# Lo parts of weights on the 256-byte grid, hi parts 96 bytes off it, and a dearer adding transfer in the plan

## The chip, the core and the metric

One program runs on one core of one Trainium2 chip. The metric is the device time of one execution in microseconds, and lower is better. Three runs of the kernel before took 527.31, 530.25 and 537.80 us; their median is 530.25 us. TensorE is called PE here, its weight loads PEld, VectorE DVE, ScalarE ACT, GpSimd POOL and SyncE SP.

## The reference

Attention with 2 batches, 12 heads, 448 positions and a head size of 64, whose scores are capped by a tanh, is followed by two feed-forward layers with their own weights, each 768 to 2048 to 768, over all 896 tokens. All is float32.

```python
scores = cap * np.tanh(scale * (q @ k.T) / cap)
x = softmax(scores) @ v                      # 896 x 768 after the heads are put side by side
h = x @ w1_in;  x = (s * np.maximum(h, 0)**2 + b) @ w1_out
h = x @ w2_in;  out = (h * np.clip(h + 3, 0, 6) / 6) @ w2_out
```

## The kernel before, in words

**The attention** runs first, to about 91 us into the span. It is not touched by the change, except that ACT and DVE already unpack the first weight columns beside it.

**The two feed-forward layers** make up the rest. A float32 number is kept as two tiles of the format fp32r that PE reads in one pass: hi is the number rounded, lo is what is left. A product of a weight block and an activation block is three matmuls into one PSUM bank, in `matmuls` (line 300): lo weight by hi activation, hi weight by lo activation, hi weight by hi activation. Each has a weight load of 128 by 128 before it and a moving stream of 448 columns, 1,792 bytes in a partition, one batch's tokens. There are 710 such products, so 2,130 matmuls, all on line 303. The matrix products are taken in a scheme that forms a two-by-two block product from seven products instead of eight; it adds and subtracts blocks of weights on DVE (line 614), and blocks of activations with transfers on POOL's queue that add into their destination (`accumulate`, line 781; there are 52), or on DVE (line 780).

**A weight's way.** A transfer on SP's queue lands it in `raw`; ACT rescales the upper half of the bits (line 285) and ACT or DVE bring the rest (lines 289, 293, 298); the float32 result f is then split by `parts` (line 600): ACT rounds f into a new tile h (line 603), and DVE writes f minus h over f itself (line 604). So h holds the hi part, and f's place becomes the lo part.

**The places in the memory** are handed out by `Space.take` (line 75) in two large areas. Places for 448 columns of activations begin on a grid of `LINE` = 64 elements, 256 bytes, counted from the area's start. All longer places, those of weights, f and h alike, begin `OFFSET` = 24 elements, 96 bytes, off that grid. A block of 128 weight columns is 512 bytes, so each block that PE loads is off the grid by the same 96 bytes, and each moving stream is on it.

**The order of the work** is written by a planner, `Plan.order` (line 125), before the program is built. It plays the tasks through with a cost for each, four queues (PE, DVE, ACT, and one for all transfers) and the memory places, and starts on each engine the ready task with the earliest due time. PE takes its products from a list, and may pull one ahead of up to 35 others that aren't ready. A task of another engine is taken as done `LAG` later than its end. An adding transfer holds the transfer queue for `SUM_COST` and lands `SUM_LATE` after that. The engines then work their instructions off strictly in this written order; the planned times don't exist on the chip.

**The squares** of the first layer's activations (`activation`, line 674) are made by DVE in one instruction (line 690), or, for the column blocks named in `SQUARES`, by ACT in two (lines 687, 688).

Of the kernel before, what the change touches and what calls it, by code (L numbers as in the profile page):

```python
# [16 lines left out]
B, H, S, D = 2, 12, 448, 64  # L17
# [7 lines left out]
BL = HK * 128  # L25
CI = KD * 128
# [3 lines left out]
SCALE = 1.0 / D**0.5  # L30
FIRST = 3
PLAIN = 4
SQUARES = (5, 6, 7, 9, 11)
HEAD = 2.0

NEGATIVE = tuple(range(HK, KD)) + tuple(range(KD, KD + HK))
LOAD = 0.004, 2.5
AHEAD = {"ACT": 30.0}
SUM_COST, SUM_LATE = 1.37, 3.5
STORE_LATE = 3.0  # L40
PIECE = 0.602
SEVENS = 2, 2
# [1 line left out]
LOWS = (True, True, False, False)  # L44

LINE, OFFSET = 64, 24
SPACE = 36 * S + 12 * CI + OFFSET, 49 * S + 6 * CI + OFFSET
OUT_ORDER = (0, 3, 1, 4, 2, 5)


class Res:


    def __init__(self, kind, tile=None, n=S, at=None):
        self.kind, self.tile, self.left, self.held, self.order = kind, tile, 0, tile is not None, None
        self.n, self.at, self.low = n, at, None


class Space:
# [12 lines left out]
                return  # L72
        raise RuntimeError("not free")

    def take(self, n):
        for area in ((1, 0) if n == S else (0, 1)):
            for a, b in self.free[area] if n == S else reversed(self.free[area]):
                at = a + (-a) % LINE if n == S else b - n - (b - n - OFFSET) % LINE
                if a <= at and at + n <= b:
                    self.cut(area, at, n)  # L80
                    return area, at
        return None
# [19 lines left out]
class Plan:  # L102


    LAG = 0.35
    WINDOW = 36

    def __init__(self, sizes):
# [2 lines left out]
    def add(self, engine, cost, run, after=(), use=(), soon=None):  # L111
        t = Task(engine, cost, run, after, list(use), len(self.tasks))
        for u in t.use:
            u.left += 1
        for a in t.after:
            a.then.append(t)
        t.soon = soon
        self.tasks.append(t)
        return t

    def order(self):
# [3 lines left out]
        for t in reversed(self.tasks):  # L125
            for s in t.then:
                t.due = min(t.due, s.due - t.cost - t.late - self.LAG)
        made = {}
# [4 lines left out]
        for t in reversed(self.tasks):  # L133
            if t.engine != "PE":
                for s in t.then:
                    t.due = min(t.due, s.due - t.cost - t.late - self.LAG)
        free = dict(self.sizes)
        space = Space(SPACE, {(*u.at, u.n) for t in self.tasks for u in t.use if u.kind == "mem" and u.held} | set(self.taken))
        banks, seen = 0, {}
# [22 lines left out]
        while left:  # L162
            moved = True
            while moved:
                moved = False
                for e, queue in waiting.items():
                    if idle[e] > now + 1e-9:
                        continue
                    for t in queue[:self.WINDOW] if e == "PE" else queue:
                        if e in AHEAD and now < t.due - AHEAD[e]:  # L170
                            continue
                        if any(a.end is None or a.end + (0 if a.engine == e and e != "DMA" else self.LAG) > now + 1e-9 for a in t.after):
                            continue
                        want = [u for u in t.use if not u.held]
                        need = {}
                        ok = True
                        for u in want:
                            if u.kind == "mem":
                                need[u] = space.take(u.n)
                                ok = need[u] is not None  # L180
                            else:
                                ok = free[u.kind] > 0 and (u.kind != "bank" or u.order == next_bank)
                                if ok:
                                    need[u] = u.kind
                                    free[u.kind] -= 1
                            if not ok:
                                break
                        if not ok:
                            for u, k in need.items():
                                if u.kind != "mem":  # L190
                                    free[k] += 1
                                elif k is not None:
                                    space.give(*k, u.n)
                            continue
                        for u, k in need.items():
                            u.held = True
                            if u.kind == "mem":
                                u.at = k
                            elif k == "bank":
                                next_bank += 1  # L200
                        t.start, t.end = now, now + t.cost + t.late
                        idle[e] = now + t.cost
                        ends.append(t)
                        queue.remove(t)
                        left -= 1
                        moved = True
                        break
            times = [x for x in idle.values() if x > now + 1e-9]
            times += [t.due - AHEAD[e] for e in AHEAD for t in waiting[e] if t.due - AHEAD[e] > now + 1e-9]
            times += [t.end + self.LAG for t in done[-80:] + ends if t.end + self.LAG > now + 1e-9]  # L210
            if not times:
                stuck = {e: [(t.name if hasattr(t, "name") else t.number, [a.number for a in t.after if a.end is None]) for t in q[:3]] for e, q in waiting.items()}
                raise RuntimeError(f"plan stuck at {now}: {free} {stuck}")
            now = min(times)
            for t in [t for t in ends if t.end <= now + 1e-9]:
                ends.remove(t)
                done.append(t)
                for u in t.use:
                    u.left -= 1
                    if u.left == 0 and u.kind == "mem":  # L220
                        space.give(*u.at, u.n)
                    elif u.left == 0:
                        free[u.kind] += 1
# [11 lines left out]
def attention_moe_moe(ctx: ExitStack, tc: tile.TileContext, qk, v, cap, w1i, w1o, s, b, w2i, w2o, out):  # L235
    nc = tc.nc
    placed = [0]
    first_area = ctx.enter_context(tc.tile_pool(name="ma", bufs=1))
    first_area.tile([128, SPACE[0]], F32, name="ma")
    first_area.seal()  # L240
    areas = [nc.sbuf_base - 4 * SPACE[0]]

    def view(at, n, dt=F32):

        placed[0] += 1
        return nc.alloc_sbuf_tensor_at(f"m{placed[0]}", (128, n), dt, offset=areas[at[0]] + 4 * at[1])[:, :]
# [18 lines left out]
    xf = [view(a, S) for a in xf_at]  # L265
    top_of = lambda n: (0, SPACE[0] - n)
    f_at = [top_of((i + 1) * CI) for i in range(FIRST + 1)]
    h_at = [top_of((i + FIRST + 2) * CI) for i in range(FIRST + 1)]
    fa_at, fb_at = top_of(8 * CI + 4 * BL), top_of(8 * CI + 7 * BL)

    def raw_tile():
        return wp.tile([128, CI, 2], U32, name="raw", tag="raw", bufs=3)
# [32 lines left out]
    at = tc.alloc_tile_pool(name="at", bufs=3)  # L305
# [146 lines left out]
    def take(p):  # L452

        xu[p] = xf[p]
        nc.vector.tensor_copy(xu[p], pav.pop(p)[:, :S])
# [70 lines left out]
    def feed_forward():  # L526
# [6 lines left out]
        def res(n=S):  # L533
            return Res("mem", None, n)
# [6 lines left out]
        def low_of(f):  # L541
            if f.low is None:
                f.low = view(f.at, f.n, F32R)
            return f.low
# [7 lines left out]
        def t_of(r, dt=F32):  # L552
            if r.tile is None:
                r.tile = view(r.at, r.n, dt)
            return r.tile
# [44 lines left out]
        def parts(f, after, before=()):  # L600

            h = res(f.n)
            a = add("ACT", acts(f.n), lambda: nc.scalar.copy(t_of(h, F32R), f.tile), after, [f, h])  # L603
            c = add("DVE", dve(f.n), lambda: nc.vector.tensor_sub(low_of(f), f.tile, h.tile.bitcast(F32)), [a, *before], [f, h])  # L604
            return (h, f), [a, c]
# [25 lines left out]
        def out_block(layer, mt, half):  # L631
            f = res(2 * CO)
            g, tasks = parts(f, [convert(w_src(layer, 1, (mt, 2 * half + i)), CO, f, i * CO, low=False) for i in range(2)])
            return g, 0, tasks
# [39 lines left out]
        def activation(layer, f, bi, c_psum, made, c_slot=None):  # L674
# [9 lines left out]
            a = add("ACT", acts(S, layer), relu, made, [src_res, t] if t is not src_res else [t], soon)  # L684
            on_act = layer == 0 and f in SQUARES
            if on_act:
# [324 lines left out]
    with tc.manual_schedule():  # L1011
# [57 lines left out]
        for p in range(P - 2):  # L1069
            at_step(U * (p // 2) + 6 + 3 * (p % 2), take, p)  # L1070
# [85 lines left out]
```

## Time and profile before

| what | value |
|---|---|
| median of three runs | 530.25 us (527.31 to 537.80) |
| profiled execution | 533.35 us, its span 531.6 us |
| PE busy in the span | 519.9 us, 98% |
| weight loads busy | 427.8 us, 80% |
| DVE, ACT, POOL busy | 443.8, 417.8, 46.7 us |
| granted TensorE clock, mean of the span | 0.999 |

A matmul's busy time overlaps the next one's, so 98% says only that PE seldom stands still. The pace at which matmuls follow each other has to be read from the count in a stretch of time.

### The profile page before, as it was taken

To read this page: it belongs to the slowest core of one execution; us is meant where nothing else is said; L and a number is where in the kernel's file an instruction comes from. 1 tells how busy PE (TensorE), PEld (TensorE's weight loads), DVE (VectorE), ACT (ScalarE), POOL (GpSimd) and SP (SyncE) were. 2 spreads that over 40 slices of the span, in tenths; PEclk is the share of its full clock that TensorE was granted. 3 is DMA by queue.
4 is the path that set the end of the run, shared out by engine and by line. 5 is a ranking of instruction groups with operands and counts; after the bars stand their busy time and mean duration, and the time that the engine had idled before them with its cause. 6 is when DMAs were issued, how large, how long until landed. Compare 5 with 4: busy or idle time off the path is not lost.

```text
span 531.6 us, 7389 instructions
## 1 busy us (share of the span) xinstructions
PE 519.9 (98%) x2720; PEld 427.8 (80%) x2720; DVE 443.8 (83%) x673; ACT 417.8 (79%) x574; POOL 46.7 (9%) x62
## 2 busy tenths in 40 slices
PE   8999999999999999999988999999999999999997
PEld 3232335999899999999978998999999999999996
DVE  2789999999987838989979999999866699799732
ACT  6999999698876849899969999854577887799610
POOL 0000000350000000001432210000000000035100
PEclk9999999999999999999999999999999999999999
DMA  8846411794237514325897743222676213279611
GB/s 308 330 124 195 130 36 50 218 190 121 81 113 261 189 51 139 120 80 144 169 288 148 172 111 100 80 80 81 210 258 203 80 48 102 91 188 174 158 56 69
DMA packets 25286, 76.31 MB, mean 144 GB/s; under 512 B 3234, under 2 KB 13218, under 8 KB 25122
## 3 DMA queue, kind: packets, MB, share of 16 engines
q1 hardware_dynamic: 17616, 63.75, 36.3%
q0 software_dynamic: 7488, 11.93, 13.5%
q8 instruction: 21, 0.34, 0.3%
q10 hardware_dynamic: 146, 0.16, 0.1%
q14 instruction: 15, 0.12, 0.1%
HBM read 61.11 MB, written 2.79 MB: 120 GB/s over the span
## 4 chain that ended last, share of the span: by engine, by line
PE 53%; DVE 12%; ACT 7%; issue 3%; DMA 2%; POOL 0%; DVEq 0%; POOLq 0%; ACTq 0%
PE pf L303 24%; PE pav L303 21%; PE pz L303 8%; DMA m<-m 2%; DVE m L298 2%; DVE m L604 2%; DVE m L690 2%; DVE m L704 1%; ACT m L603 1%; ACT m L285 1%; DVE m L793 1%; DVE m L293 1%; ACT raw L289 1%; DVE m L614 1%; DVE m L796 1%
## 5 line engine op out<-in xcount | busy, mean ns | idle before, releaser
L303 PE MATMUL pf<-m,m 128*128 128x448 f32 x1053 | 224.0, 366 | 3.2 <-ACT pf L867 1.6
L303 PEld LDWEIGHTS pf<-m,m 128*128 128x128 f32 x1053 | 197.0, 188 | 21.6 <-ACT pf L867 2.0
L303 PE MATMUL pav<-m,m 128*128 128x448 f32 x813 | 173.6, 365 | 0.5 <-DVE pav L739 0.5
L303 PEld LDWEIGHTS pav<-m,m 128*128 128x128 f32 x813 | 152.3, 188 | 13.9 <-DVE pav L739 0.9
L298 DVE SCALAR_TENSOR_TENSOR m<-raw,m 128x512 uint32<-128x512 uint32 (+1 forms) x123 | 92.4, 764 | 14.1 <-ACT raw L289 12.2
L604 DVE TENSOR_TENSOR m<-m,m 128x1024 fp32r<-128x1024 f32 (+2 forms) x56 | 79.6, 1425 | 15.6 <-ACT m L603 15.5
L603 ACT CAST m<-m 128x1024 fp32r<-128x1024 f32 (+2 forms) x56 | 68.2, 1220 | 27.2 <-DVE m L298 15.8
L781 POOL DMA_DIRECT2D m<-m x52 | 45.9, 943 | 450.1 <-DVE m L692 152.2
L289 ACT ACTIVATE raw<-raw 128x768 uint16<-128x768 uint16 (+1 forms) x37 | 67.9, 1834 | 0.7
L285 ACT ACTIVATE m<-raw 128x512 f32<-128x512 f32 (+1 forms) x79 | 60.0, 766 | 10.7 <-DMA raw<-in_w2o 2.8
L303 PE MATMUL pz<-m,m 128*128 128x448 f32 x264 | 57.7, 366 | 0.2 <-DVE m L604 0.2
L303 PEld LDWEIGHTS pz<-m,m 128*128 128x128 f32 x264 | 49.4, 187 | 4.7 <-DVE m L604 0.5
L293 DVE TENSOR_SCALAR m<-m 128x512 uint32<-128x512 uint32 (+1 forms) x80 | 37.4, 475 | 4.5 <-ACT m L285 4.4
L349 ACT ACTIVATE t<-t 128x896 f32<-128x896 f32 x42 | 39.9, 949 | 1.2
L344 ACT ACTIVATE t<-ps 128x896 f32<-128x896 f32 x42 | 37.8, 901 | 3.6 <-PE ps L336 3.6
L336 PE MATMUL ps<-rqk 64*128 64x448 f32 x144 | 34.1, 576 | 1.1 <-ACT t L344 1.0
L362 PE MATMUL pav<-t,va 128*64 128x448 f32 x144 | 31.9, 555 | 0.2 <-ACT t L349 0.2
L336 PEld LDWEIGHTS ps<-rqk 64*128 64x128 f32 x144 | 11.5, 185 | 22.9 <-ACT t L344 12.8
L614 DVE TENSOR_TENSOR m<-m 128x384 f32<-128x384 f32 (+1 forms) x46 | 26.0, 566 | 1.5 <-PE pf L303 0.7
L362 PEld LDWEIGHTS pav<-t,va 128*64 128x64 f32 x144 | 8.4, 136 | 20.1 <-issue 15.4
L704 DVE SCALAR_TENSOR_TENSOR m<-m,bt,m 128x448 fp32r<-128x448 f32 x32 | 21.5, 681 | 3.3 <-ACT m L698 2.5
L793 DVE SCALAR_TENSOR_TENSOR m<-m,m 128x448 fp32r<-128x448 f32 x31 | 19.0, 620 | 4.7 <-DMA m<-m 2.4
(135 smaller groups left out, 422.8 us busy)
## 6 DMA issues: line engine op xcount, KB each, us to landing
raw<-in_w1i SPq DMA_DIRECT2D x16, 768.0 KB, 5.1
raw<-in_w1o SPq DMA_DIRECT2D x24, 512.0 KB, 3.9
raw<-in_w2i SPq DMA_DIRECT2D x16, 768.0 KB, 5.0
raw<-in_w2o SPq DMA_DIRECT2D x24, 512.0 KB, 4.0
m<-m POOLq DMA_DIRECT2D x52, 224.0 KB, 4.1
rqk<-in_qk SPq DMA_DIRECT2D x11, 448.0 KB, 4.7
out<-m SPq DMA_DIRECT2D x12, 224.0 KB, 1.9
rb<-rows SPq DMA_DIRECT2D x10, 224.0 KB, 3.8
```

Source lines behind the costliest of these rows:

```text
L285: nc.scalar.activation(bits, up, AF.Copy, scale=2.0**-112)
L289: nc.scalar.activation(by[:, :, 2], by[:, :, 1], AF.Copy, scale=2.0**-13, bias=0.5**14 - 0.5)
L293: nc.vector.tensor_scalar(bits, bits, 3, None, op0=ALU.logical_shift_left)
L298: nc.vector.scalar_tensor_tensor(out=bits, in0=part, scalar=29 if low else mask, in1=bits, op0=ALU.logical_shift_right if low else ALU.bit ...
L303: nc.tensor.matmul(ps[:, :S], w[a], rhs[r], start=start and i == 0, stop=stop and i == 2, skip_group_check=True)
L336: nc.tensor.matmul(ps[:, j, :S], raw_qk[p][rows, 1, c * 128:(c + 1) * 128], raw_qk[p][rows, 0, :], start=True, stop=True)
L344: nc.scalar.activation(u_t[n], u_ps.pop(n)[:, :, :S], AF.Tanh, scale=icap_r)
L349: nc.scalar.activation(u_t[n], u_t[n], AF.Exp, scale=cap_r)
L362: nc.tensor.matmul(pav[p][(top, end)[j], :S], va[bi][:, d, (2 * (p % 2) + j) * NC + c, :], u_t[n][:, j, :], start=(p % 2 == 0 and c == 0), ...
L603: a = add("ACT", acts(f.n), lambda: nc.scalar.copy(t_of(h, F32R), f.tile), after, [f, h])
L604: c = add("DVE", dve(f.n), lambda: nc.vector.tensor_sub(low_of(f), f.tile, h.tile.bitcast(F32)), [a, *before], [f, h])
L781: t = add("DMA", SUM_COST, lambda: nc.gpsimd.dma_start(out=r.tile, in_=other.tile, accum_op=ALU.add), after, [r, other])
```

## The change

Places for weights can now be asked for with a shift: `parts` sets 24 elements for h, the hi part, and every other weight place, so f with the later lo part, gets 0 and begins on the 256-byte grid. The early weights, whose places are written out by hand, follow the same rule, for which both areas end 40 elements later. So of each product's three weight loads one (lo) is now on the grid and two (hi) are 96 bytes off it, as before.

In the planner an adding transfer holds the queue for 1.6 instead of 1.37, the lag after another engine's task is 0.4 instead of 0.35, and block 6 of the squares moves from ACT to DVE.

```diff
-SQUARES = (5, 6, 7, 9, 11)
+SQUARES = (5, 7, 9, 11)
...
-SUM_COST, SUM_LATE = 1.37, 3.5
+SUM_COST, SUM_LATE = 1.6, 3.5
...
-SPACE = 36 * S + 12 * CI + OFFSET, 49 * S + 6 * CI + OFFSET
+SPACE = 36 * S + 12 * CI + LINE, 49 * S + 6 * CI + LINE
...
-        self.n, self.at, self.low = n, at, None
+        self.n, self.at, self.low, self.shift = n, at, None, 0
...
-    def take(self, n):
+    def take(self, n, shift):
...
-                at = a + (-a) % LINE if n == S else b - n - (b - n - OFFSET) % LINE
+                at = a + (-a) % LINE if n == S else b - n - (b - n - shift) % LINE
...
-    LAG = 0.35
+    LAG = 0.4
...
-                                need[u] = space.take(u.n)
+                                need[u] = space.take(u.n, u.shift)
...
-    h_at = [top_of((i + FIRST + 2) * CI) for i in range(FIRST + 1)]
-    fa_at, fb_at = top_of(8 * CI + 4 * BL), top_of(8 * CI + 7 * BL)
+    h_at = [top_of((i + FIRST + 2) * CI + LINE - OFFSET) for i in range(FIRST + 1)]
+    fa_at, fb_at = top_of(8 * CI + LINE + 4 * BL), top_of(8 * CI + LINE + 7 * BL)
...
             h = res(f.n)
+            h.shift = OFFSET
```

The new costs move instructions. Two places matter to the prediction.

ACT at the end of the first layer, some 270 to 281 us into the span before, where the last sums of activations are split into hi parts (lines 789 and 792) and a bank is seeded for the next block by a copy (line 867). Before:

```order
L792 ACTIVATE m_2526<-m_2238 128x448
L603 CAST m_2532<-m_2405 128x1536
L982 ACTIVATE m_2548<-pz 128x448
L792 ACTIVATE m_2554<-m_2220 128x448
L982 ACTIVATE m_2561<-pav 128x448
L789 ACTIVATE m_2566<-m_1920,bt 128x448
L982 ACTIVATE m_2570<-pf 128x448
L792 ACTIVATE m_2577<-m_2369 128x448
L982 ACTIVATE m_2584<-pav 128x448
L867 COPY pf<-pf 128x448
```

And with the change, where line numbers from 603 on are one higher:

```order
L793 ACTIVATE m_2527<-m_2225 128x448
L983 ACTIVATE m_2538<-pz 128x448
L790 ACTIVATE m_2545<-m_1900,bt 128x448
L604 CAST m_2552<-m_2389 128x1536
L983 ACTIVATE m_2563<-pav 128x448
L793 ACTIVATE m_2571<-m_2213 128x448
L983 ACTIVATE m_2576<-pf 128x448
L983 ACTIVATE m_2581<-pav 128x448
L868 COPY pf<-pf 128x448
L793 ACTIVATE m_2594<-m_2367 128x448
```

The rounding of a large weight tile (the cast of 1,536 columns) has moved from ahead of the second line to behind the biased split, and one split of a sum has moved from ahead of the seeding copy to behind it.

PE at the same place: products of three matmuls, named by bank, activation and weight tile. Before:

```order
L303 MATMUL pf<-m_2554,m_2348 128x448
L303 MATMUL pf<-m_2575,m_2327 128x448
L303 MATMUL pf<-m_2554,m_2327 128x448
L303 MATMUL pf<-m_2526,m_2348 128x448
L303 MATMUL pf<-m_2537,m_2327 128x448
L303 MATMUL pf<-m_2526,m_2327 128x448
L303 MATMUL pf<-m_2566,m_2418 128x448
L303 MATMUL pf<-m_2582,m_2346 128x448
L303 MATMUL pf<-m_2566,m_2346 128x448
```

And with the change:

```order
L303 MATMUL pf<-m_2527,m_2346 128x448
L303 MATMUL pf<-m_2543,m_2325 128x448
L303 MATMUL pf<-m_2527,m_2325 128x448
L303 MATMUL pav<-m_1968,m_2568 128x448
L303 MATMUL pav<-m_2026,m_2552 128x448
L303 MATMUL pav<-m_1968,m_2552 128x448
L303 MATMUL pf<-m_2571,m_2346 128x448
L303 MATMUL pf<-m_2586,m_2325 128x448
L303 MATMUL pf<-m_2571,m_2325 128x448
```

A product of the next block (into pav, with the weights that the moved cast makes) has come in between the last two products of this group, whose two places are exchanged.

## Rows read from the trace of the kernel before

**Rows 1.** Page: the span and busy time of the engines.
```profile
span 531.6 us, 7389 instructions
PE 519.9 (98%) x2720; PEld 427.8 (80%) x2720; DVE 443.8 (83%) x673; ACT 417.8 (79%) x574; POOL 46.7 (9%) x62
```

**Rows 2.** Page: groups by line; busy us, mean ns of one | idle before.
```profile
L303 PE MATMUL pf<-m,m 128*128 128x448 f32 x1053 | 224.0, 366 | 3.2 <-ACT pf L867 1.6
...
L303 PE MATMUL pav<-m,m 128*128 128x448 f32 x813 | 173.6, 365 | 0.5 <-DVE pav L739 0.5
...
L303 PE MATMUL pz<-m,m 128*128 128x448 f32 x264 | 57.7, 366 | 0.2 <-DVE m L604 0.2
L303 PEld LDWEIGHTS pz<-m,m 128*128 128x128 f32 x264 | 49.4, 187 | 4.7 <-DVE m L604 0.5
```

**Rows 3.** Stretches, line 303 alone: us, PE and PEld busy (count), clock, DMA.
```profile
86.00:329.00 243.00, 235.98 (x1172) 219.17 (x1171) 1.00 0.56 150
330.00:528.00 198.00, 197.75 (x957) 178.84 (x956) 1.00 0.44 125
...
142.00:246.00 104.00, 104.00 (x522) 97.59 (x521) 1.00 0.42 138
252.00:274.00 22.00, 22.00 (x112) 20.65 (x111) 1.00 0.94 221
284.00:328.00 44.00, 44.00 (x222) 41.31 (x222) 1.00 0.59 147
332.00:526.00 194.00, 194.00 (x941) 175.76 (x940) 1.00 0.44 126
```

**Rows 4.** The chain that ended last: start us, us, what.
```profile
162.65 10.80 PE pf L303 x54
...
463.90 9.30 PE pav L303 x45
```

**Rows 5.** Waits of PE: waited for, us in total, times, longest.
```profile
PE pf L303 <- ACT pf L867: 1.6, 1, 1.6
...
PE pf L303 <- DVE m L793: 1.3, 1, 1.3
...
PE pav L303 <- DVE pav L739: 0.5, 1, 0.5
...
PE pf L303 <- ACT m L792: 0.2, 1, 0.2
PE pz L303 <- DVE m L604: 0.2, 1, 0.2
```

**Rows 6.** Timeline of ACT, 270 to 281 us: start, us, instruction, idle before.
```profile
270.96 1.46 ACT L603 CAST m<-m 128x1536 fp32r<-128x1536 f32 x1
...
278.07 0.67 ACT L789 ACTIVATE m<-m,bt 128x448 fp32r<-128x448 f32 x1 [1.72 <-DMA m<-m]
278.65 0.53 ACT L982 ACTIVATE m<-pf 128x448 f32<-128x448 f32 x1
279.17 0.58 ACT L792 ACTIVATE m<-m 128x448 fp32r<-128x448 f32 x1
279.65 0.52 ACT L982 ACTIVATE m<-pav 128x448 f32<-128x448 f32 x1
280.07 0.54 ACT L867 COPY pf<-pf 128x448 f32<-128x448 f32 x1
```

**Rows 7.** Groups of the squares on ACT and DVE, columns as in Rows 2.
```profile
L690 DVE SCALAR_TENSOR_TENSOR m<-m,st 128x448 f32<-128x448 f32 x22 | 14.8, 678 | 0.0
...
L688 ACT ACTIVATE m<-m,st 128x448 f32<-128x448 f32 x10 | 6.7, 670 | 0.3
...
L687 ACT ACTIVATE m<-m 128x448 f32<-128x448 f32 x10 | 5.8, 577 | 0.2
```

**Rows 8.** Page: issues of adding transfers, KB each, median us to landing.
```profile
m<-m POOLq DMA_DIRECT2D x52, 224.0 KB, 4.1
```

## The prediction

> **What bounds the kernel now.** I read the page's busy times first. PE is busy for 519.9 of 531.6 us [rows 1], so only two things can change the time much: the pace of its matmuls, and the few places where it stands still. The groups by line come next: the three groups of line 303 hold 1053 + 813 + 264 = 2,130 matmuls [rows 2], all of one shape, and fill the span from about 86 to 528 us [rows 3]. Their mean duration of 366 ns is no pace, since they overlap.
>
> The pace is read from stretches in which PE never waits. From 142 to 246 us there are 104.0 us and 522 matmuls, where the count takes in those cut by the two ends, about two; so 104.0 / 520 = 0.200 us each. From 332 to 526 us it is 194.0 / 939 = 0.2066 us [rows 3]. The chain of waits says it without ends: 54 matmuls in 10.80 us are 200.0 ns each, 45 in 9.30 us are 206.7 ns [rows 4]. So there are **two paces**, 200.0 and 206.7 ns, and the granted clock is 1.00, the 2.4 GHz level, in both. 1,173 matmuls (2,130 less 957) stand before 329.5 us, nearly all at the fast pace, and 957 behind it at the slow one [rows 3]. Between lies one short wait of PE, for line 604 [rows 5]. After the earlier waits the fast pace came back: 252 to 274 us gives 22.0 / 110 and 284 to 328 us gives 44.0 / 220, both 0.200 [rows 3]. A weight load takes 187 ns [rows 2], and loads are busy for 97.59 of 104 us at the fast pace and 175.76 of 194 us at the slow one [rows 3]: the load is no longer there, only the gap to the next.
>
> The profiled execution took 533.35 us. At the fast pace throughout it would be 957 x 6.7 ns = 6.4 us shorter, 526.95 us; at the slow pace throughout 1,173 x 6.7 ns = 7.9 us longer, 541.2 us. The three runs, 527.31 to 537.80 us, lie between these. I take it that they differ mainly in how long each ran at which pace. The profiled execution lies 3.1 us above the median, so about half of its slow share is typical.
>
> Last, the waits of PE within line 303 sum to 1.6 + 1.3 + 0.5 + 0.2 + 0.2 = 3.8 us [rows 5]; more than that is not to be had from the plan.
>
> **The change, part by part.**
>
> *Places of the lo parts.* Nothing is added to PE: 2,130 loads and 2,130 matmuls remain. 710 of the loads now begin on the grid. The trace has no matmul of line 303 with a weight there, so the price has to be bounded. Nearest from above: every load of the product keeps or takes the slow pace, +7.9 us against the profiled execution. Nearest from below: every matmul runs at the fast pace, -6.4 us. Further down, no row excludes that one more step of 6.7 ns goes from the 710 lo matmuls (-4.8 us more) or from all 2,130 (-14.3 us more); further up the 710 could take one more step, +4.8 us over the slow pace.
>
> I take **-6.4 us**, the fast pace throughout. Places alone don't set the pace, since one set of places showed both; a pace is something that the stream falls into, and it left the slow one after all waits but the last [rows 3]. At the slow pace it stayed for 957 matmuls in a row, each with the same distance between its load's place and its stream's. With the change this distance changes twice in every three matmuls, so a pace that lives from repeating itself has less to hold on to, and 200.0 is the one that was found again more often. That is an inference, not a row, and its chance below is accordingly small.
>
> Against it speaks the Trainium skill, "TensorE: Matmul & The Clock Gate", section "Step-by-step: what each phase is for": PE has two independent SBUF read ports, one for the moving stream and one for weight loads, and loading the next weights takes no read bandwidth from the running matmul. By it the place of a weight changes nothing, and this term of the sum is 0 instead of -6.4 us. The trace neither bears it out nor refutes it, since no load of line 303 has another place.
>
> *Addresses in ACT's and DVE's work.* The same instructions of the same sizes run on f and h; no cost is taken, and DVE has idle time in the span [rows 1].
>
> *SUM_COST and LAG.* These make no instruction; they move some. PE's largest waits, 1.3 us for line 793 and 1.6 us for line 867 [rows 5], lie at one place, 275 to 281 us. Before, ACT stands there for 1.72 us before line 789 until a transfer lands, then needs 0.67 for it, 0.53, 0.58 and 0.52 for three more, and only then comes the seeding copy at 280.07 us [rows 6]. With the change one split (0.58 us) is behind the copy, and PE has a product of the next block to do meanwhile, three matmuls or 0.6 us. But the cast of 1,536 columns, 1.46 us [rows 6], is now between line 789 and the copy, as are one more bank copy (0.52) and one other split (0.58). If line 789 still waits until 278.07 us, the copy comes 1.46 + 0.52 + 0.58 - 0.58 = 2.0 us later, and PE, with 0.6 us of other work, stands 1.4 us longer. If the places handed out anew, or the earlier stand of line 789 in ACT's order, end that wait, up to 3.8 us go. The adding transfers keep their order there, and take a median of 4.1 us to land [rows 8], so nothing makes them earlier by itself. I take **0**, between +1.4 and -3.8, as neither end has the better row. What is late next in the good case is DVE's line 793, whose own 1.3 us of PE's wait [rows 5] stays.
>
> *Squares of block 6.* Two batches: ACT loses 2 x (577 + 670) = 2.5 us, DVE gains 2 x 678 = 1.4 us [rows 7]. PE's only wait near there is 0.5 us for DVE's line 739 [rows 5]; one square of 0.68 us ahead of it would make it 1.2, none would leave it. Bounds -0.5 and +0.7 us, taken as **0**. The cover is PE's list, in which a product's results are used many products later; without it the 1.4 us on DVE would count.
>
> *Sum.* 533.35 - 6.4 + 0 + 0 = 526.95, so **527.0 us**, 0.6% under the median of 530.25 us.
>
> **The rivals.** About 2% of the median, 10.6 us, is what can be told from no change here; so faster means under 519.6 us and slower over 540.9 us.
>
> *Forecast, the fast pace holds: 0.38.* 527.0 us, and with the bounds of the plan's terms 523 to 529 us.
>
> *The place of a weight does nothing: 0.31.* The change then doesn't do what it says, the two paces share the matmuls by chance as before, and the time lies between 525 and 540 us, most likely near the median, 530 us. For it: one set of places showed both paces [rows 4]. Against it: nothing in the rows. This is the rule of "TensorE: Matmul & The Clock Gate" on the two read ports.
>
> *A pace below 200 ns: 0.17.* If the 710 lo matmuls lose one more step the time is 526.95 - 4.8 = 522.2 us; if all do, 512.7 us. For it: a load takes only 187 ns [rows 2], so 13 ns of each 200 are neither load nor needed by the next load. Against it: no stretch without a wait ran under 0.200 us [rows 3]. The Trainium skill, same page, section "Back-to-back issue gap", gives columns / 2.4 + 2.5 ns for matmuls that follow each other, which is 189.2 ns for 448 columns; by that estimate the time would be 526.95 - 2,130 x 10.8 ns = 503.9 us. The rows disagree with it at both paces.
>
> *Slower, the lo loads drag the stream into the slow pace: 0.14.* The place is each product's first matmul: its load from the grid runs beside a moving stream on the same grid. If these two meet, one step of 6.7 ns is lost there, and the stream stays at the slow pace for the next two, as it did for 957 matmuls [rows 3]. All slow gives 541.2 us; with one step more for the 710 it is 546.0 us. It decides from the point where more than the lo third is slow: the third alone, 710 x 6.7 = 4.8 us over 526.95, is 531.7 us, no change. Against it: with the old places the stream also left the slow pace.
>
> **How the numbers follow.** The predicted time is the forecast's 527.0 us. Under 513.5 us lies the all-lower case with the page's, about 0.10; over 538.5 us lie the slow rival's upper part and the far end of the second case, about 0.11. So the range is 513.5 to 538.5 us. The forecast's own range is 523 to 529 us. Faster by over 2%: from the third case the part in which all matmuls lose a step, 0.11, and 0.03 for that together with a gain in the plan, so 0.14. Slower: the dragged stream at 541.2 us or more, 0.09, since a part of it ends just under the bound. Within 2%: 0.77.
>
> **What would show it.** In stretches without a wait, line 303 counts 0.200 us a matmul everywhere, 332 to 526 us included, where it was 0.2066. If a stretch there shows 0.2066 again, the second case holds; 0.2022 (one slow in three) or 0.1978 (one faster in three) would show that the place of the load itself has a price. For the plan's terms: PE's waits for lines 793 and 867, now 794 and 868, are again together 2 to 4 us, and the cast of 1,536 columns stands ahead of the seeding copy. The prediction is wrong if a pace other than the two appears, or if PE's waits sum to more than 6 us.

## The result and the profile after

Over 20 runs the changed kernel took a median of 533.61 us (530.35 to 537.10). Run beside it, the kernel before took 535.00 us (20 runs, 527.31 to 537.94; the 530.25 us shown ahead of the prediction was a median of three). The ratio that belongs to the verdict is 1.0058 [1.0034, 1.0083]: no change by the measure of 2%, and slower by a little, where the prediction had faster by a little. That ratio leaves out runs over 1.5% above the fastest of the same kernel, which takes 10 of the 20 runs of before and none of the change's, so I set all runs beside it: with those of the later experiments, 44 of the change have a mean of 533.43 us and 136 of before 533.57 us, ratio 0.9997 [0.9982, 1.0013]. The kernels are equal in the mean; they differ in how their runs spread. Before's fall into two groups, 59 of 136 under 532.5 us (mean 529.75) and nearly all others at 534 to 540 (mean 536.50); of the change's, 17 of 44 are under 532.5.

The profiled execution of the changed kernel took 530.96 us, so it belongs to the lower group. The page's span and busy times, against [rows 1]:
```profile
span 529.2 us, 7398 instructions
PE 515.2 (97%) x2720; PEld 428.2 (81%) x2720; DVE 446.0 (84%) x675; ACT 415.8 (79%) x570; POOL 46.8 (9%) x62
```
The groups of line 303, against [rows 2]; busy us, mean ns of one | idle before:
```profile
L303 PE MATMUL pf<-m,m 128*128 128x448 f32 x1041 | 219.2, 363 | 2.5 <-DVE m L605 1.6
...
L303 PE MATMUL pav<-m,m 128*128 128x448 f32 x825 | 174.2, 363 | 2.7 <-DVE m L605 2.1
...
L303 PE MATMUL pz<-m,m 128*128 128x448 f32 x264 | 57.0, 363 | 1.0 <-DVE m L605 1.0
L303 PEld LDWEIGHTS pz<-m,m 128*128 128x128 f32 x264 | 49.5, 188 | 4.5 <-DVE m L605 1.4
```
The 2,130 matmuls are there again. A load takes 188 ns, 187 before. Stretches without a wait, line 303 alone, columns as in [rows 3]:
```profile
222.00:246.00 24.00, 24.00 (x122) 22.53 (x121) 1.00 0.37 115
...
400.00:440.00 40.00, 40.00 (x202) 37.56 (x201) 1.00 0.42 143
...
480.00:524.00 44.00, 44.00 (x222) 41.31 (x221) 1.00 0.52 115
```
With the two that the ends cut taken off, 40.00 / 200 and 44.00 / 220 are 0.200 us: in this execution the stretch after 332 us, 0.2066 before [rows 3], runs at the fast pace. The chain of waits agrees, against [rows 4] (start us, us, what):
```profile
463.49 8.40 PE pav L303 x42
...
479.69 9.60 PE pf L303 x48
```
That is 200.0 ns both times. The waits of PE within line 303, against [rows 5]:
```profile
PE pav L303 <- DVE m L605: 2.1, 1, 2.1
PE pf L303 <- DVE m L605: 1.6, 1, 1.6
...
PE pz L303 <- DVE m L605: 1.0, 1, 1.0
...
PE pf L303 <- DVE m L797: 0.5, 1, 0.5
PE pav L303 <- DVE pf L740: 0.2, 1, 0.2
PE pf L303 <- DVE pav L740: 0.2, 1, 0.2
PE pf L303 <- ACT pf L868: 0.2, 1, 0.2
PE pav L303 <- DVE m L744: 0.2, 1, 0.2
```
They sum to 6.0 us, 3.8 before [rows 5]. The waits for lines 868 (the seeding copy) and 794 have nearly gone, and DVE's line 605, the lo parts of a weight, is late in their place, three times. The timeline of ACT at the same place, against [rows 6]:
```profile
275.81 0.67 ACT L790 ACTIVATE m<-m,bt 128x448 fp32r<-128x448 f32 x1 [0.20 <-DMA m<-m]
276.38 1.46 ACT L604 CAST m<-m 128x1536 fp32r<-128x1536 f32 x1
...
281.06 0.56 ACT L868 COPY pf<-pf 128x448 f32<-128x448 f32 x1
```
The transfer that held line 789 until 278.07 us now lets line 790 begin at 275.81; the cast stands ahead of the seeding copy as foretold, and the copy comes 1.0 us later than before (281.06 after 280.07), but PE waits only 0.2 us for it. The longest of the waits for line 605 lies here too. PE's product of the next block, which the prediction counted as work to do meanwhile, needs the lo parts that DVE makes behind the moved cast:
```profile
278.19 1.75 DVE L605 TENSOR_TENSOR m<-m,m 128x1536 fp32r<-128x1536 f32 x1
279.99 0.88 PE L303 MATMUL pav<-m,m 128*128 128x448 f32 x3 [2.15 <-DVE m L605]
```

### The profile page after: what moved, and what is told of

The parts are those of the page before. It is cut to its first block, busy times and chain, and to the rows that moved or that the text cites. A ratio compares the mean times of both kernels' runs of the same rounds, so it can differ in the third digit from the quotient of the medians.

```text
span 529.2 us, 7398 instructions
## 1 busy us (share of the span) xinstructions
PE 515.2 (97%) x2720; PEld 428.2 (81%) x2720; DVE 446.0 (84%) x675; ACT 415.8 (79%) x570; POOL 46.8 (9%) x62
## 5 line engine op out<-in xcount | busy, mean ns | idle before, releaser
L303 PE MATMUL pf<-m,m 128*128 128x448 f32 x1041 | 219.2, 363 | 2.5 <-DVE m L605 1.6
L303 PEld LDWEIGHTS pf<-m,m 128*128 128x128 f32 x1041 | 194.8, 188 | 18.1 <-DVE m L605 2.0
L303 PEld LDWEIGHTS pav<-m,m 128*128 128x128 f32 x825 | 154.6, 188 | 14.4 <-DVE m L605 2.5
L793 ACT ACTIVATE m<-m 128x448 fp32r<-128x448 f32 x31 | 17.9, 585 | 9.1 <-PE pav L303 5.7
```

The source lines that it names most:

```text
L303: nc.tensor.matmul(ps[:, :S], w[a], rhs[r], start=start and i == 0, stop=stop and i == 2, skip_group_check=True)
```

## What a run's time is made of

I took 20 executions apart by the starts of their 2,130 matmuls: how many run at a slow pace and by how much; the stops, which are all that lies between neighbouring starts beyond 200 ns and isn't pace (the 3.6 us near 88 us in which PE does other matmuls are left out); and matmuls that follow at 373 ns, while the granted clock is 0.50 (the 1.2 GHz level), 0.173 us too long each. What is left is 521.0 to 522.5 us in all of them, so these three items are the difference, but for 1.5 us. Ten of them, numbers worked out from the traces:

| execution | us | slow matmuls (ns each) | stops us | at half clock |
|---|---|---|---|---|
| before | 533.35 | 957 (206.7) | 5.84 | 0 |
| before, second | 537.24 | 1,308 (206.7) | 5.07 | 8 |
| before, third | 530.0 | 0 | 6.75 | 10 |
| change | 530.96 | 75 (204.4) | 8.74 | 0 |
| change, second | 531.71 | 429 (204.4) | 7.82 | 0 |
| numbers only | 529.22 | 27 | 8.04 | 0 |
| numbers only, second | 531.91 | 666 (206.7) | 6.25 | 0 |
| places only | 531.35 | 27 (204.6) | 7.87 | 7 |
| places only, second | 536.8 | 822 (204.4) | 8.83 | 13 |
| hi on the grid | 537.38 | 1,989 (204.4) | 6.04 | 0 |

For the first row: 521.1 us and 5.84 us of stops, and 957 x 6.66 ns = 6.37 us, are 533.3 us.

## The experiments

Kernels of one group below ran on one chip, beside runs of the kernel before there. In the texts on record "the plan's numbers" are SQUARES, SUM_COST and LAG together.

**The two halves of the change, and all parts on the grid (12 runs each; before: median 535.28 of 35).** A copy of the kernel before, the numbers alone, the places alone, and the kernel before with OFFSET at 0, so that hi and lo lie on the grid:
```diff
# numbers only (on before)          # places only (on the change)
-SQUARES = (5, 6, 7, 9, 11)         -SQUARES = (5, 7, 9, 11)
+SQUARES = (5, 7, 9, 11)            +SQUARES = (5, 6, 7, 9, 11)
-SUM_COST, SUM_LATE = 1.37, 3.5     -SUM_COST, SUM_LATE = 1.6, 3.5
+SUM_COST, SUM_LATE = 1.6, 3.5      +SUM_COST, SUM_LATE = 1.37, 3.5
-    LAG = 0.35                     -    LAG = 0.4
+    LAG = 0.4                      +    LAG = 0.35
# all on the grid (on before)
-LINE, OFFSET = 64, 24
+LINE, OFFSET = 64, 0
```


> The kernel before, once more, for a second trace of it. Theory A (a matmul's pace is one of two, and which one a run falls into is chance): its trace shows 200.0 and 206.7 ns again, with another share of the slow one than the 957 of 2,130 matmuls of the first trace, and its time moves by 6.7 ns for each matmul of difference, between 527 and 541 us. Theory B (the second half of this program is slow for a reason in its own work): the slow pace begins again at about 330 us, behind the wait for line 604, and the time is 533 us.

> Only the planner's numbers of the change (SUM_COST 1.6, LAG 0.4, block 6 of the squares on DVE); all weights stay 96 bytes off the grid. Theory A (places set the slow pace, the plan sets the waits): slow stretches show 206.7 ns as before, and PE's waits in line 303 sum to about 8.7 us as in the changed kernel, against 5.8 before; 2 to 4 us slower than before at the same share of the slow pace. Theory B (the plan's new order changes the pace): slow stretches show 204.4 ns as in the changed kernel.

> Only the places of the change (lo on the grid, hi 96 bytes off); the planner's numbers are those of before. Theory A (places set the slow pace): slow stretches, where there are any, show 204.4 ns a matmul (203, 204 and 206.5 within a product) instead of 206.7, the fast ones 201, 200 and 199; waits near 5.8 us; 2 to 3 us under the changed kernel. Theory B (places do nothing, the plan does all): 206.7 ns in slow stretches and no pattern of three.

> The kernel before with OFFSET = 0: all weights, hi and lo, on the 256-byte grid like the streams. Theory A (a weight's place against its stream's sets the pace): a pace other than 200.0 and 206.7 ns; if the grid is what hurts, over 206.7 ns or slow throughout, 541 us or more. Theory B (places do nothing): 200.0 and 206.7 ns by chance, 527 to 541 us.

The copy: 535.49 us (528.79 to 537.35), profiled at 537.24. Its chain shows the pace flip within one execution:
```profile
163.56 10.80 PE pf L303 x54
...
317.75 10.54 PE pf L303 x51
...
484.53 9.92 PE pf L303 x48
```
These are 200.0, 206.7 and 206.7 ns. The slow pace began at 250 us (251 to 275 us gives 24.0 / 116 = 0.207), 330 us in the first trace: no place in the program owns it.

The numbers alone: **530.02 us**, 12 of 12 runs between 529.22 and 530.56; a repeat further down gave 530.57, 11 of 12 under 532.5. All 24 against before's 136: mean 530.58 to 533.57, ratio 0.9944 [0.993, 0.996]. Each 12 runs against before on their own chip give 0.9930 [0.991, 0.995] and 0.9955 [0.993, 0.999]. In the mean this version beats both kernels, by less than the measure of 2%, and not by a faster lower group: its 23 runs under 532.5 us have a mean of 530.34, before's 59 one of 529.75. What it lacks is the upper group. The places alone: 534.06 us, 2 of 12 under 532.5; mean ratio to before 1.0005 [0.9982, 1.0027]. The change against the numbers alone: 1.0054 [1.0037, 1.0069], and on the one chip that ran both 1.0036 [1.0006, 1.0066]. So the numbers that I costed at nothing bring half a per cent, and with the places on top it is gone.

The edits of these two kernels differ in the places only, but the work on the chip does not: the planner asks which places are free, so another place writes another order. The seam of [rows 6] shows it; with the numbers alone ACT has there:
```profile
276.77 0.67 ACT L789 ACTIVATE m<-m,bt 128x448 fp32r<-128x448 f32 x1 [0.25 <-DMA m<-m]
277.34 0.52 ACT L867 COPY pf<-pf 128x448 f32<-128x448 f32 x1
...
278.23 1.47 ACT L603 CAST m<-m 128x1536 fp32r<-128x1536 f32 x1
```
The cast is behind the seeding copy, and the copy comes 2.7 us earlier than before. So the order with the cast ahead of the copy, shown in the section on the change, is not what the new costs write by themselves. Set side by side in order of time, 384 of PE's 2,130 matmuls go to another bank in the change than with the numbers alone, and 18 with the places alone than in before. What the 0.54% owes to the places themselves and what to the order is not shown. All on the grid: 534.32 us, and its chain has neither of the old paces alone:
```profile
163.90 11.16 PE pf L303 x54
...
211.02 8.68 PE pav L303 x42
...
465.13 9.12 PE pav L303 x45
```
206.7 and 206.7, then 202.7 ns; no stretch of this trace ran at 200.0.

**The change again, the places swapped, and a short pause (before: 534.91 of 29).** Swapped: the change with the hi parts on the grid and the lo parts 96 bytes off it. The pauses: after products 380, 440, 500, 560 and 620 PE does one small matmul more, with weights of zero, into the bank of the running product; it changes no value.
```diff
# swapped (on the change)
-        ... self.shift = n, at, None, 0
+        ... self.shift = n, at, None, OFFSET
-            h.shift = OFFSET
+            h.shift = 0
...
# pauses (on before; and on numbers only)
+KICKS = 380, 440, 500, 560, 620
...
+        done[0] += 1
+        if done[0] in KICKS:
+            nc.tensor.matmul(bank_of(bank)[:24, :D], marks[:, 32:56], ones, start=False, stop=True, ...)
```


> The changed kernel once more, for its spread and a second trace. Theory A (each restart of the stream after a wait picks the fast or the slow pace; with the change the slow one is 204.4 ns a matmul): the time is 530.6 us plus 4.4 ns for each matmul at the slow pace, so runs between 530.5 and 538 us, and the trace shows long stretches at 200.0 or at 204.4 ns and none at 206.7. Theory B (its slow runs come from longer waits): slow stretches stay short and PE's waits make up the difference.

> The places the other way round: hi parts on the 256-byte grid (two loads of three), lo parts 96 bytes off; the planner's numbers are the change's. Theory A (a load on the grid costs the slow pace part of its step and adds to the fast one): paces between those of the change (200.0 and 204.4 ns) and those of all weights on the grid (201 to 206.7 ns); about 532 to 537 us. Theory B (only the mixture counts, not which part is on the grid): the same paces and spread as the changed kernel.

> The kernel before with five extra small matmuls in its last half (64 columns, weights all zero, added to the bank in use, so nothing changes in the results), one every 60 products from the 380th, to break the even stream there. Theory A (the pace is picked at each restart and then kept): the picks are thrown again six times, so the times no longer fall into two groups near 530 and 537 us but spread between, and the trace changes pace at a kick. Theory B (the slow pace is a state of the whole core for the rest of the run): two groups as before, each about 1.5 us later, and no change of pace at a kick.

> The same five small matmuls in the kernel that has only the planner's numbers of the change, whose 12 runs lay between 529.2 and 530.6 us. Theory A (any restart may pick the slow pace): some runs now have slow stretches of 60 products (180 matmuls, 1.2 us each), and the spread grows to 530.5 to 537 us. Theory B (its places in the order make the fast pace sure): all runs within 1.5 us, about 1.5 us later than without the extra matmuls.

The change: 534.43 us. Swapped: 538.23 us (4 runs, 536.54 to 539.39), the slowest of all, and the chain says why:
```profile
468.30 9.20 PE pav L303 x45
484.86 9.81 PE pf L303 x48
```
204.4 ns, and so for 1,989 of the matmuls; no stretch at 200.0. The same two distances, dealt to the other parts, remove the fast pace, and up to matmul 1,863 PE's order by banks is that of the change. **So the place of a weight has a price**, shown by the one trace of this kernel and, for the pace of 204.4 ns, by those of the change and of the places alone.

The pauses: 532.84 us on before, 7 runs under 533.2 and 5 from 536.8 up; 536.82 on the numbers, 5 runs up to 533.5 and 7 from 536.4 up (530.02 without the pauses, on another chip). The stretches on both sides of the pause near 410 us, line 304 here (the diff adds a line), on before and then on the numbers:
```profile
376.00:409.00 33.00, 33.00 (x167) 30.98 (x166) 1.00 0.71 241
412.00:446.00 34.00, 34.00 (x172) 31.92 (x171) 1.00 0.29 96
```
```profile
376.00:409.00 33.00, 33.00 (x162) 29.85 (x161) 1.00 0.65 219
413.00:446.00 33.00, 33.00 (x161) 29.85 (x161) 1.00 0.28 92
```
The first kept 0.200 over the pause, the second 0.206: in these two traces all ten pauses left the pace as it was. The traced run with the pauses on the numbers has 1,086 slow matmuls, but the last slow stretch began at 332 us, ahead of the first pause; how the pauses bring more runs into the upper group is not shown.

**Pauses late only, pauses that wait for another engine, and one more trace of either kernel (before: 534.25 of 23).** The late ones are those at 500, 560 and 620, on the numbers. In the turns DVE copies 64 columns of the bank first, and PE's small matmul waits for that:
```diff
# turns (on before)
+            nc.vector.tensor_copy(turn, bank_of(bank)[:, :D])
+            nc.tensor.matmul(bank_of(bank)[:24, :D], marks[:, 32:56], turn, start=False, stop=True, ...)
```


> The planner's numbers alone, with the small matmuls only at the 500th, 560th and 620th product, behind the short wait near the 436th product (matmul 1308) that the first two, at the 380th and 440th, hid. Theory A (a pause of PE's own keeps the pace, only a wait for another engine picks it anew; the wait at matmul 1308 is what saves the kernel with the planner's numbers from slow second halves): all runs within 1.5 us again, about 530 to 531 us. Theory B (any extra matmul disturbs the pace): two groups, 531 and 537 us, as with five.

> The kernel before with five round trips in the last half at the same five products: DVE copies 64 columns of the bank, and the small zero-weight matmul reads that copy, so PE waits for DVE each time. Theory A (a wait for another engine picks the pace anew): where PE waits, the trace may go from one pace to the other, unlike at the small matmuls alone, where it never did; the times no longer fall into two groups but spread, 5 to 8 us above the fast runs of before for the waits themselves. Theory B (the pace of the second half is settled at matmul 1173): no change of pace at any of the five.

> One more look at the changed kernel, for a trace of a run of its upper group (533 to 537 us). Theory A: its time is near 530.6 us plus 4.4 ns for each matmul in stretches at 204.4 ns, which then begin at a wait. Theory B: its slow runs differ by longer waits, with the pace at 200.

> One more look at the kernel before, for a trace of either group. Theory A: time and slow matmuls agree with the other two traces of it, 533.35 us with 957 slow and 537.2 us with 1,308 slow, at 6.7 ns each, so about 527 to 529 us where none is slow. Theory B: the groups differ by more than the pace.

Late pauses: 535.17 us, 4 runs at 530.7 to 531.6, two at 534 and 6 at 536.3 to 537.7. My idea that a fast choice at the last wait holds for the rest **fell**: up to product 500 this is the kernel that gave 12 runs in 12 under 531, and 8 of its 12 runs are above 533 us. But the numbers alone never ran on this chip, and the one traced run, 531.55 us, is of the lower group, so what the upper one is made of was not seen. Turns: 535.36 us (533.54 to 538.56, no two groups). In its trace a slow pace held from a gap of 0.05 us at 359 us to the turn at 374 us, and the fast one behind it (line 305 here):
```profile
364.00:373.00 9.00, 9.00 (x46) 8.09 (x44) 1.00 0.24 93
376.00:409.00 33.00, 33.00 (x167) 30.97 (x166) 1.00 0.69 229
```
9.00 / 44 to 45 is slow, 33.00 / 165 is 0.200. So at a wait for another engine the pace can change, but the turns didn't bring all runs down. Nor does a change of pace need a wait. The same trace, columns as in [rows 3]:
```profile
150.00:204.00 54.00, 54.00 (x272) 50.69 (x271) 1.00 0.50 166
204.00:208.00 4.00, 4.00 (x21) 3.71 (x20) 1.00 0.65 147
208.00:276.00 68.00, 68.00 (x330) 61.53 (x330) 1.00 0.58 153
```
54.00 / 270 is 0.200 and 68.00 / 328 is 0.207. In between PE is busy throughout, no two starts lie more than 207 ns apart, and the slow pace that begins there, at 206.4 us, lasts 345 matmuls.

The third trace of the change, 531.9 us, is of the lower group again, with 537 slow matmuls at 204.4 ns. The third trace of before, 530.0 us, shows the third item, at the place of [rows 5] and [rows 6]. Stretches of line 303, then PE's waits there:
```profile
276.00:280.00 4.00, 2.22 (x7) 1.15 (x6) 0.86 0.97 186
280.00:284.00 4.00, 2.63 (x7) 2.38 (x8) 0.50 0.71 118
284.00:288.00 4.00, 4.00 (x17) 3.65 (x17) 0.79 0.69 115
```
```profile
PE pf L303 <- ACT pf L867: 1.6, 1, 1.6
PE pf L303 <- DVE m L793: 1.1, 1, 1.1
```
There are two long waits with five matmuls between them. The granted clock falls to 0.50 behind the first and ahead of the second, and stays there for 6.8 us:
```profile
278.00:279.00 1.00, 0.88 (x4) 0.84 (x5) 0.93 1.16 204
279.00:280.00 1.00, 0.73 (x2) 0.12 (x1) 0.50 0.48 82
```
The numbers alone have there:
```profile
276.00:280.00 4.00, 3.16 (x16) 2.62 (x15) 1.00 1.08 304
280.00:284.00 4.00, 3.75 (x19) 3.16 (x18) 1.00 0.53 91
```
No stretch at half clock is in any of the ten traces with the new numbers; of the eight with the old ones six have it, though not before's first, whose waits were nearly the same [rows 5]. Nor is a pair of waits enough in the change: four of its traces have two waits of 0.8 to 1.5 us there, and none a stretch at half clock. The mean granted clock speaks for the untraced runs too (in the traces it is 0.9968 or less with such a stretch, 0.9987 or more without): it is under 0.9985 in 92 of 116 runs of before, 15 of 44 of the change, and 1 of 24 of the numbers alone.

**The numbers apart, and the rest (before: 534.59 of 29).** SUM_COST at 1.6 alone; LAG at 0.4 with the new SQUARES; the numbers and the change again.

> The planner's numbers alone, again, on whatever chip this call gets. Theory A (its 12 runs between 529.2 and 530.6 us were luck or that session's; any wait may pick the slow pace): two groups now, 529 to 531 us and 534 to 538 us, like the same kernel with late small matmuls. Theory B (its order makes the fast pace sure): all 12 runs within 1.5 us again.

> The changed kernel beside it on the same chip. Theory A: 530 to 537 us, and a trace with slow stretches at 204.4 ns; a trace of a run above 533 us has over 600 matmuls in them. Theory B (the waits of its plan vary from run to run and make the upper group): a run above 533 us with under 300 slow matmuls.

> The kernel before with SUM_COST = 1.6 alone. Theory A (the dearer adding transfer is what breaks up the two long waits near 276 and 280 us): no stretch at the half clock near 280 us, and waits near 315 and 332 us longer, as with all three numbers. Theory B (LAG and the squares do it): a half-clock stretch in two of three traces and the waits of before, 5.8 us less the half clock.

> The kernel before with LAG = 0.4 and block 6 of the squares on DVE, without the dearer adding transfer. Theory A: the two long waits near 276 and 280 us stay, with or without the half clock; the small waits near 124, 141 and 147 us of the changed kernel appear. Theory B: the waits of the changed kernel at 315 and 332 us appear.

Numbers again 530.57, change again 532.43 us (profiled at 531.87 with 420 slow). SUM_COST alone: 534.07 us (4 runs, 533.46 to 534.59), profiled with 57 slow matmuls but stops of 11.27 us, the most of all. Two of its waits, 1.3 and 0.9 us for line 604 between 310 and 340 us, stand where the change waits for line 605, so that lateness comes with SUM_COST; with the other two numbers one such wait of 0.3 us is there. LAG and SQUARES: 533.43 us, again two groups (527.92 to 536.65), profiled with 1,092 slow. Neither half does it; only with all three numbers were nearly all runs (23 of 24) under 532.5 us.

**Two last traces for the change's upper group.**

> The changed kernel, one more trace, in the hope of its upper group, which none of its four traces shows. Theory A: above 533 us it has 700 or more matmuls at 204.4 ns and PE's other waits stay between 7.8 and 8.8 us. Theory B: above 533 us with fewer than 550 slow matmuls, and longer waits.

> The places alone, one more trace: 10 of its 12 runs were above 532.5 us, its one trace was not (531.35 us, 27 slow matmuls). Theory A: above 532.5 us its stretches at 204.4 ns are long, at 4.4 ns for each matmul over 522 us plus the waits and any half-clock stretch. Theory B: the waits or the half clock make its upper group.

The change came at 531.62 us, a fifth execution from its lower group, so its upper group was never traced. The places alone came at 536.8, and there it is seen:
```profile
468.02 9.20 PE pav L303 x45
484.58 9.81 PE pf L303 x48
```
204.4 ns from 362 us to the end, 822 matmuls, 3.7 us, and the half clock as in before:
```profile
280.00:284.00 4.00, 3.59 (x10) 2.67 (x9) 0.61 0.58 108
284.00:288.00 4.00, 2.77 (x9) 2.27 (x10) 0.81 0.59 97
```

## Why the prediction was wrong

The bound it started from held: two paces at a granted clock of 1.00, 200.0 and 206.7 ns, and the spread of before's runs being mostly their share. Its limits for before, 526.95 and 541.2 us, contain all 136 runs. The time, 533.61 us, lies in the range; the forecast of 527.0 us does not hold.

**The step that failed is the term of the places, "I take -6.4 us, the fast pace throughout".** Alone they moved the mean by +0.05% [-0.18, +0.27], some 0.3 us; on top of the numbers, with the order that they bring along, they cost 0.54% [0.37, 0.69], 2.9 us. The reason given for it, that a slow pace "lives from repeating itself" and has less to hold on to when the distance changes within a product, is refuted: with the distance changing within every product slow stretches lasted some 350 matmuls (change, second) and 822 (places only, second), and the swapped kernel, which mixes as much, was slow throughout. The other reason, that the stream "left the slow one after all waits but the last", misreads [rows 3]: the stretches ahead of those waits were at 0.200 too, so nothing there was left; the only long slow stretch of that trace was entered once and kept to the end. What the places do is smaller: within a product the matmuls follow at 201, 200 and 199 ns where the stream is fast, at 203, 204 and 206.5 where it is slow. The slow pace costs 4.4 ns instead of 6.7, the fast one nothing; but the change's runs are under 532.5 us no more often than before's. Over the 957 slow matmuls of before's profiled execution that would be worth 957 x 2.2 ns = 2.1 us, a third of what I took, and only if there were no more of them.

Here the Trainium skill's page "TensorE: Matmul & The Clock Gate", section "Step-by-step: what each phase is for", with its two independent SBUF read ports, was the rule against the change, since by it loading the next weights takes no read bandwidth from the running matmul. The times agree with the 0 that the prediction drew from it in so far as the places alone gained nothing. That a place does nothing, which the page doesn't say in these words, the traces contradict: 204.4 instead of 206.7 ns with the lo parts on the grid, no 200.0 with the hi parts or all of them there, with loads of 187 to 188 ns as before. The same page's "Back-to-back issue gap" gives the formula behind the 189.2 ns for the isolated gap of one matmul and says that in a stream of load and matmul pairs both set the spacing, so the prediction took it for a stream that it isn't meant for; no stretch without a wait of any of the 20 traces ran under 200 ns a matmul.

**SUM_COST and LAG, "I take 0", was mis-sized too, and its order is not that of these two numbers alone.** With the numbers alone the seam at 275 to 281 us came near the good end: line 789 was held 0.25 us instead of 1.72, and of 3.1 us of waits [rows 5] 1.0 us were left. In the change, with the cast ahead of the copy, the three matmuls taken as cover for 0.6 us waited themselves, 2.1 us for line 605; 2.3 us were left in the profiled execution, and the waits for lines 794 and 868, said to be 2 to 4 us again, were 0.2. Line 605 became late elsewhere as well, which the prediction did not name: 2.6 us in the change besides the seam, 2.3 in the numbers alone. PE's waits sum to 6.0 us, not 3.8, and the stops to 8.74 after 5.84. At +2.9 us, or +2.2 over five traces of the change and three of before, this is beyond my bound of +1.4. Against that the kernel with the numbers alone lacks two items which I hadn't priced: the half clock, 1.2 to 2.4 us where it occurs (7 to 14 matmuls), and, as far as the times of its runs tell, most of the long slow stretches. In sum 0.56%, 3.0 us of the mean. That a wait of the plan could set the pace of what follows stood in [rows 3], since the change of pace there lies at a wait, and I used it only to describe.

**Squares, 0.** Right in size: PE's wait for line 739, 0.5 us [rows 5], is now twice 0.2 for line 740.

**The rivals.** "The place of a weight does nothing", 525 to 540 us, most likely near the median, has the time, but not the mechanism. "A pace below 200 ns" did not come: 199 ns is one matmul in three, beside 201. "The lo loads drag the stream into the slow pace", with 541 us and more, did not come: slow stretches at 204.4 ns exist, but the five traces of the change, all of the lower group, have most matmuls at the fast pace, and its longest run took 538.21 us. Of the tests of the last part one spoke: a pace other than the two appeared, 204.4 ns (neither of the 202.2 and 197.8 that I had named for a price of the place). PE's waits came to 6.0 us, at the limit that I had set and not over it.

**What stays open.** Why the stream takes one pace or the other; load time (187 to 188 ns) and granted clock (1.00) are the same in both. Most long slow stretches begin and end at a wait, and a gap of 0.05 us can do it, but two changes had none: that of the turns at 206.4 us, and in the second trace of the numbers alone the end of 642 slow matmuls at 280.2 us. Why late pauses, and the places, bring more runs of the numbers' kernel into the upper group, and whether the places do it by themselves or by the order that the planner then writes. Whether the change's upper group is slow stretches at 204.4 ns, as in the one trace of the places alone: 13 of its 27 runs there have a mean granted clock under 0.9985, so for the others it isn't the half clock; that is all the runs show.

## What to carry to other kernels

Where a bound engine shows two paces without a wait, look at what each change of pace follows; a plan's order can then be worth more or less than its waits, and a term that moves only an order can't be costed at its waits alone. Measure the parts of a change apart: here one gained 0.56% and with the other 0.54% was lost, and the pair looked like nothing. Then check that a part's edit moves only what it names: here a shift of places also changed the order of the work. With run times in two groups, three runs say little.

## What the runs showed of the chip

- Pairs of a 128x128 weight load and a 448-column matmul run at 200.0 or at 206.7 ns, with loads of 187 to 188 ns and a granted clock of 1.00 in both. The pace changed at waits for another engine (in the turns at 374 us), in the turns at 206.4 us also without any, and held over all ten pauses of PE itself in two traces.
- The place of the weights against that of the stream, in steps of 96 bytes on a grid of 256, went with a slow pace of 204.4 ns (lo on the grid), with the loss of the fast one (hi on the grid, 204.4 in 1,989 of 2,130), and with 206.7 and then 202.7 ns (all on the grid); the last two rest on one trace each.
- At two waits of 1.1 and 1.6 us with five matmuls between, the granted clock fell to 0.50, the 1.2 GHz level, behind the first wait and for 6.8 us, in which ten matmuls followed at 373 ns; at the like pair in another execution of the same program it stayed at 1.00.
